# Adding the two halves of a norm's sum: small copies and an add on VectorE or GpSimd instead of a TensorE product

## The chip, the cores and the metric

The kernel runs on one core of a Trainium2 chip. The metric is device time in microseconds (us) for one execution. Before the change the median of three runs is 1548.53 us (1548.2 to 1552.75). The profile comes from one further execution of 1549.24 us, of which 1547.5 us lie between its first and its last instruction (the span).

## What is computed

A linear attention over 8 batches, 8 heads, 576 positions and a head size of 64, with a norm over the head size, and behind it two feed-forward layers over 4608 tokens (width 512, hidden width 2048). All is float32.

```
kv  = einsum('bhsd,bhse->bhde', k, v)
out = einsum('bhsd,bhde->bhse', q, kv)
rms = sqrt(mean(out * out, axis=-1, keepdims=True) + 1e-06)
x   = out / rms * g_norm          # as [4608, 512]
h = x @ moe_w_in;   r = maximum(h, 0);   x = (s * (r * r) + b) @ moe_w_out
h = x @ moe2_w_in;  x = (h / (1 + exp(-h))) @ moe2_w_out
```

## The kernel before

The tokens are cut into nine blocks of 512 columns: block t holds the first 512 positions of batch t, and the ninth block (t = 8) the remaining 64 positions of all eight batches. Products that need float32 are made of three passes with each operand split into a rounded half and a rest (mm3, lines 207 to 210).

Attention goes by pairs of heads: four pairs for each batch (attention_pair). For each pair TensorE makes kv (L532), the output o (L208 to L210 into o_ps) and the output of the last 64 positions (L566 into r_ps, copied out to orem by ScalarE or VectorE, L231 or L233). Then normalize follows, with two heads of 64 on the 128 partitions:

- sq (L628, ScalarE) squares o;
- part (L633, VectorE) adds the squares over groups of 32 partitions. It leaves 128 x 16 numbers, in which a head's sum is spread over two groups of 32 partitions;
- ms (L640, TensorE) adds the two groups of each head: a product with the constant matrix pairs_of, 128 x 128 by 128 x 16, into PSUM;
- rms (L644, ScalarE) takes the root, inv (L647, VectorE) the reciprocal, spread (L652, VectorE) turns it back to 128 x 512, and x (L659, VectorE) multiplies.

normalize runs 36 times: for the four pairs of batch 0 (where the flag z is true), for 28 pairs of batches 1 to 7, and four times for the ninth block (last_block). The four of batch 0 lie in the first 30 us, the other 32 between 50 us and 450 us.

In the same stretch TensorE works on blocks 0 to 4 of the first layer (unit: mm1 into h, mm2 into acc, both by L208 to L210), while ScalarE, VectorE and GpSimd turn the squares (L786, L789, L216, L222), decode weights (L309 to L332) and build sums and differences of weight quarters (L399, L413, L214, L220). From about 450 us on the other blocks go in pairs, by a scheme with seven instead of eight block products (hidden, L980; outputs, L1121 to L1123; results, L1157). The second layer's weights are decoded up to about 854 us.

The order on every engine is worked out before the launch by a planner (class Plan). Each step is added with its engines and a duration for each, a key, what it needs and makes, and the buffers it takes and gives back. The planner walks through time with these durations; a step goes to the engine on which it can start first, or, where the duration is marked Port, on which it ends first, and steps marked Port aren't planned beside one another. Each engine then runs its own list strictly in that order. So another step or another duration early in the program can change every list behind it.

PSUM tiles of the pool `at` (two buffers) are taken by a pair's kv, by the o of batches 1 to 7, by r and by ms. Before the change ms took a buffer of this pool, so it could wait until an earlier one had been copied out.

Of the kernel before, what the change touches and what calls it, by code (L numbers as in the profile page):

```python
# [8 lines left out]
F32 = mybir.dt.float32  # L9
F32R = mybir.dt.float32r  # L10
U32 = mybir.dt.uint32
AF = mybir.ActivationFunctionType
ALU = mybir.AluOpType
# [6 lines left out]
class Plan:  # L20
# [19 lines left out]
    def add(self, engines, key, fn, needs=(), makes=(), takes=(), gives=(), move=None, opens=(), until=None):  # L40
        self.ops.append((key, len(self.ops), engines, fn, needs, makes, takes, gives, move, opens, until))
        for b in gives:
            self.users[b] = self.users.get(b, 0) + 1
# [90 lines left out]
def kernel(  # L134
# [21 lines left out]
    nc = tc.nc  # L156
    B, H, S, D = q.shape
    NT, DM = out.shape
    DFF = w_in1.shape[1]
    P = 128  # L160
# [4 lines left out]
    T = NCH * P  # L165
    REM = S - T
    Q = 32
# [28 lines left out]
    ap = st_ap.enter_context(tc.tile_pool(name="ap", bufs=1))  # L196
    dr = ctx.enter_context(tc.tile_pool(name="dr", bufs=1, space=bass.MemoryType.DRAM))
    ps = ctx.enter_context(tc.tile_pool(name="ps", bufs=1, space=bass.MemoryType.PSUM))
    eng = {"PE": nc.tensor, "ACT": nc.scalar, "DVE": nc.vector, "POOL": nc.gpsimd, "SP": nc.sync}
# [24 lines left out]
    def copy(e, dst, src, factor=None):  # L224
        if factor is not None:
            if e == "ACT":
                nc.scalar.activation(dst, src, AF.Identity, scale=factor)  # L227
            else:
                eng[e].tensor_scalar(dst, src, factor, None, op0=ALU.mult)
        elif e == "ACT":  # L230
            nc.scalar.copy(dst, src)  # L231
        else:
            eng[e].tensor_copy(dst, src)  # L233

    def dma(dst, src):
        nc.sync.dma_start(out=dst, in_=src)  # L236
# [10 lines left out]
    add = plan.add  # L247
    ACT, DVE, POOL = "ACT", "DVE", "POOL"

    def psum(b, name):  # L250
        return ps.tile([P, T], F32, tag=plan.place[b], name=name)
# [10 lines left out]
    def act(n):  # L262
        return {ACT: 0.1 + n * 0.83e-3}

    def dve(n):
        return {DVE: 0.07 + n * 1.05e-3}
# [176 lines left out]
    def new_x(t):  # L443
        x_t[t] = xp.tile([P, KD, T], F32, tag="x32", name="x32")
# [3 lines left out]
    def attention_pair(bb, p, key, before=None):  # L448
# [150 lines left out]
        else:  # L599
# [14 lines left out]
        add({"SP": 0.48}, key + 2.4, lambda e: dma(orem_d[:, p, bb, :], st["orem"]), needs=[f("ro")],  # L614
            makes=[f("orem")], gives=[b["orem"]], move=0.18)
        normalize(bb, p, key + 2, [f("o")], [b["pso"]] + [b["qT"]] * z, lambda: st["pso"])

    def normalize(t, p, key, needs, gives, src):

        z = t == 0  # L620
        st = {}
        me = (t, p)
        f = lambda name: (name, t, p)
        psm = ("at", ("m", me))

        def sq(e):
            st["sq"] = lent["z", p][:, :T] if z else ap.tile([P, T], F32, tag="sq", name="sq")
            nc.scalar.activation(st["sq"], src(), AF.Square)  # L628

        def part(e):  # L630

            st["part"] = ap.tile([P, T // Q], F32, tag="part", name="part", bufs=2)
            nc.vector.tensor_reduce(  # L633
                out=st["part"], in_=st["sq"].rearrange("p (b r) -> p b r", r=Q), op=ALU.add,
                axis=mybir.AxisListType.X, apply_transpose=True,
            )

        def ms(e):
            st["ps"] = psum(psm, "m_ps")
            nc.tensor.matmul(st["ps"][:, :T // Q], pairs_of, st["part"], start=True, stop=True)  # L640

        def rms(e):
            st["rms"] = ap.tile([P, T // Q], F32, tag="rms", name="rms", bufs=2)
            nc.scalar.activation(st["rms"], st["ps"][:, :T // Q], AF.Sqrt, bias=eps, scale=1.0 / D)  # L644

        def inv(e):
            nc.vector.reciprocal(st["rms"], st["rms"])  # L647

        def spread(e):

            st["inv"] = st["sq"]
            nc.vector.transpose(  # L652
                st["inv"].rearrange("p (b d) -> p b d", d=Q), st["rms"].unsqueeze(2).to_broadcast([P, T // Q, Q])
            )

        def x(e):
            if t < TP and p == 0:
                new_x(t)
            nc.vector.scalar_tensor_tensor(  # L659
                out=x_t[t][:, p] if t < TP else st["sq"], in0=src(), scalar=gn, in1=st["inv"], op0=ALU.mult, op1=ALU.mult  # L660
            )

        add(act(T), key, sq, needs=needs, makes=[f("sq")], takes=[] if z else [("sq", me)])
        add(dve(T), key + 0.2, part, needs=[f("sq")], makes=[f("part")], takes=[("part", me)])
        add({"PE": 0.2}, key + 0.4, ms, needs=[f("part")], makes=[f("ms")], takes=[psm], gives=[("part", me)])
        add({ACT: 0.16}, key + 0.5, rms, needs=[f("ms")], makes=[f("rms")], takes=[("rms", me)], gives=[psm])
        add({DVE: 0.17}, key + 0.6, inv, needs=[f("rms")], makes=[f("inv")])
        add(dve(T), key + 0.7, spread, needs=[f("inv")], makes=[f("spread")], gives=[("rms", me)])
        add(dve(T), key + 0.8, x, needs=[f("spread"), ("gn",)] + ([("x32", t, p - 1)] if p else []), makes=[("x32", t, p)],
            takes=[("x32", t)] if t < TP and p == 0 else [], gives=[("sq", me)] * (0 < t < TP) + gives)  # L670
        if t >= TP:
            add({"SP": 0.48}, key + 0.9, lambda e: dma(x1_d[t - TP, :, p], st["sq"]), needs=[("x32", t, p)], makes=[("x1", t, p)],
                gives=[("sq", me)], move=0.73)

    def last_block(key):
        t = NB - 1
        for p in range(NP):
            st = {}
            qb = ("qT", (t, p))

            def load(e, p=p, st=st):
                st["x"] = ap.tile([P, S], F32, tag="qT", name="qT")
                dma(st["x"][:, :T], orem_d[:, p].rearrange("p b s -> p (b s)"))

            add({"SP": 0.48}, key - 1 + p * 0.1, load, needs=[("orem", bb, p) for bb in range(B)] + [("xl", t, p - 1)] * (p > 0),
                makes=[("xl", t, p)], takes=[qb], move=0.73)
            normalize(t, p, key + 0.5 + 0.7 * p, [("xl", t, p)], [qb], lambda st=st: st["x"][:, :T])
# [502 lines left out]
    with tc.manual_schedule():  # L1190
# [5 lines left out]
        eps, gn, s_t, b_t, sgn, mag_s, root, guess, b1, b_neg, g0 = (vecs[:, i:i + 1] for i in range(11))  # L1196
# [19 lines left out]
        for i in range(2):  # L1216
            nc.vector.tensor_tensor(
                pairs_of.rearrange("p (h i d) -> p h i d", h=2, d=Q)[:, :, i], quarters[:, :, 0], quarters[:, :, 1],
                op=ALU.add,
# [40 lines left out]
        for m in range(KF):  # L1260
            for kind in "io":
                to, tag = wanted[2 * m + (kind == "o")], f"w{kind}{m}"
# [19 lines left out]
        def turn2(e):  # L1282
# [4 lines left out]
            needs=[("x1", t, p) for p in range(NP) for t in range(TP, NB)] + [("x32", NB - 1, p) for p in range(NP)], makes=[("l2p",)],  # L1287
            gives=[("xr", x) for x in P_RING])
# [6 lines left out]
        for b_, x in new + [(("xr", x), x) for x in P_RING]:  # L1295
            plan.settle(b_, x)
        add({POOL: 0.0}, KF * (TP - 2) + 12, turn3,
            needs=[("wd", n, l, kind, j) for n in range(8) for l in range(2) for kind in "io" for j in range(NS) if (n, l) != (A21, 0)],
            makes=[("l2q",)], gives=[b_ for b_, _ in new])
# [23 lines left out]
        for i in range(350):  # L1323
            add({"PE": 0.11 * (2 if i < 17 else 1)}, 1e6 + i,
                warm_up,
                takes=[("acc", "warm")] * (i == 0), gives=[("acc", "warm")], until=40)
# [51 lines left out]
```

## Time and profile before

| | |
|---|---|
| median of three runs | 1548.53 us |
| the profiled execution, and its span | 1549.24 us, 1547.5 us |
| TensorE busy | 1536.7 us (99%) |
| VectorE, ScalarE, GpSimd busy | 70%, 55%, 41% |
| DMA engines, mean | 233 GB/s |
| TensorE's share of the chain that ended last | 88% |

An engine's busy time is the union of its instructions' records. A matmul's end is modelled: one of 512 columns is drawn 0.39 us long while the next starts 0.23 us later, so the distance of two starts is what a matmul costs. PEld is the loading of weights into TensorE; it runs beside the matmul in front. A float32 product that isn't split by the program stands as two loads and two matmuls, so the 32 products of the change are 64 records.

### The profile page before, as it was taken

What the parts mean: (1) busy time and instruction counts of PE and PEld (TensorE: products, weight loads), DVE (VectorE), ACT (ScalarE), POOL (GpSimd) and SP (SyncE); (2) the same over time, 40 slices, a digit from 0 to 9 for tenths busy, and PEclk for the clock granted to TensorE, in tenths of its full rate; (3) what the DMA queues carried; (4) which work ended last, traced back from release to release, by engine and by line L of the source; (5) the groups of instructions that cost most, each with busy time, mean ns of one, the idle gap of its engine ahead of it and who ended that gap; (6) DMA issues with size and microseconds to landing.
All of it is one profiled execution on the core that took longest, in us unless ns stands there. A gap on an engine that the chain in (4) does not pass through costs nothing.

```text
span 1547.5 us, 23039 instructions
## 1 busy us (share of the span) xinstructions
PE 1536.7 (99%) x7402; PEld 1255.4 (81%) x7402; DVE 1084.1 (70%) x1908; ACT 855.9 (55%) x1683; POOL 634.4 (41%) x584
## 2 busy tenths in 40 slices
PE   9999999999999999999999999999999999999999
PEld 6778888887888888888888788888888888888887
DVE  6887787877677587888888766765676666666521
ACT  6886566566576586667665444544444344544222
POOL 2331122111125144578457823762376246622410
PEclk9999999999999999999999999999999999999999
DMA  8866789988466788897988876877677766876684
GB/s 220 214 188 197 218 253 285 280 233 243 164 217 231 254 254 261 281 310 249 333 277 289 259 239 192 264 189 252 190 258 189 250 196 218 189 254 200 198 197 150
DMA packets 343496, 361.22 MB, mean 233 GB/s; under 512 B 166480, under 2 KB 228944, under 8 KB 343376
## 3 DMA queue, kind: packets, MB, share of 16 engines
q1 hardware_dynamic: 343248, 359.76, 76.4%
q8 instruction: 59, 0.97, 0.3%
q14 instruction: 61, 0.50, 0.1%
q0 software_dynamic: 128, 0.00, 0.0%
HBM read 272.63 MB, written 87.03 MB: 232 GB/s over the span
## 4 chain that ended last, share of the span: by engine, by line
PE 88%; DMA 4%; DVE 3%; ACT 2%; SPq 1%; issue 1%; POOL 1%; POOLq 0%; ACTq 0%; DVEq 0%
PE hp L980 28%; PE acc L1121 10%; PE acc L1123 10%; PE acc L1122 10%; PE h L208 5%; PE h L210 4%; PE h L209 4%; PE acc L208 4%; PE acc L209 4%; PE acc L210 4%; DMA raw<-in_moe_w_out_dram 1%; PE kv_ps L532 1%; PE acc L820 1%; PE acc L819 1%; PE acc L821 1%; SPq L236 1%
## 5 line engine op out<-in xcount | busy, mean ns | idle before, releaser
L980 PE MATMUL hp<-xo,win 128*128 128x512 f32 x2016 | 510.6, 390 | 1.8 <-DVE tmp L1005 1.8
L980 PEld LDWEIGHTS hp<-xo,win 128*128 128x128 f32 x2016 | 378.0, 188 | 84.1 <-DVE tmp L1005 5.9
L220 POOL TENSOR_TENSOR g<-tmp,g 128x512 fp32r<-128x512 f32 x192 | 249.7, 1308 | 309.4 <-ACT g L214 277.7
L1121 PE MATMUL acc<-g,wout 128*128 128x512 f32 x672 | 262.0, 390 | 0.8 <-DVE ya L1132 0.5
L1123 PE MATMUL acc<-g,wout 128*128 128x512 f32 x672 | 261.8, 390 | 0.0
L1122 PE MATMUL acc<-g,wout 128*128 128x512 f32 x672 | 261.7, 389 | 0.0
L1130 DVE TENSOR_TENSOR ya<-acc,ya 128x512 f32<-128x512 f32 x168 | 115.6, 688 | 126.9 <-PE acc L1123 117.8
L1121 PEld LDWEIGHTS acc<-g,wout 128*128 128x128 f32 x672 | 126.1, 188 | 27.9 <-DVE ya L1132 0.9
L1123 PEld LDWEIGHTS acc<-g,wout 128*128 128x128 f32 x672 | 126.3, 188 | 26.4
L1122 PEld LDWEIGHTS acc<-g,wout 128*128 128x128 f32 x672 | 126.3, 188 | 26.2
L214 ACT ACTIVATE g<-tmp 128x512 fp32r<-128x512 f32 x192 | 119.4, 629 | 26.3 <-PE acc L1123 11.7
L208 PE MATMUL acc<-gh,wo 128*128 128x512 f32 x320 | 132.2, 413 | 0.4 <-ACT y L227 0.4
L786 ACT ACTIVATE h<-h 128x512 f32<-128x512 f32 x96 | 56.0, 583 | 131.9 <-PE h L210 131.3
L208 PE MATMUL h<-xh,wi 128*128 128x512 f32 x320 | 126.7, 396 | 0.1
L1157 POOL TENSOR_TENSOR ya<-ya 128x512 f32<-128x512 f32 x84 | 108.2, 1318 | 45.1 <-DVE ya L1130 35.6
L210 PE MATMUL h<-xh,wi 128*128 128x512 f32 x320 | 125.2, 391 | 0.0
L210 PE MATMUL acc<-gh,wo 128*128 128x512 f32 x320 | 125.2, 391 | 0.0
L209 PE MATMUL acc<-gh,wo 128*128 128x512 f32 x320 | 125.1, 391 | 0.0
L209 PE MATMUL h<-xl,wi 128*128 128x512 f32 x320 | 124.9, 390 | 0.0
L332 POOL TENSOR_TENSOR rq<-raw 128x256 uint32<-128x256 uint32 x68 | 43.5, 640 | 189.5 <-DVE raw L318 101.1
L1005 DVE TENSOR_TENSOR tmp<-hp,tmp 128x512 f32<-128x512 f32 x144 | 98.8, 686 | 24.5 <-PE hp L980 23.1
L214 ACT ACTIVATE rq<-rq 128x256 fp32r<-128x256 f32 x192 | 77.5, 413 | 63.4 <-POOL rq L332 28.9
(170 smaller groups left out, 2649.4 us busy)
## 6 DMA issues: line engine op xcount, KB each, us to landing
wout<-wo SPq DMA_DIRECT2D x368, 256.0 KB, 4.2
win<-wi SPq DMA_DIRECT2D x144, 512.0 KB, 5.1
wi<-rq SPq DMA_DIRECT2D x96, 256.0 KB, 3.7
wo<-rq SPq DMA_DIRECT2D x96, 256.0 KB, 3.4
win<-wi SPq DMA_DIRECT2D x80, 256.0 KB, 4.2
raw<-in_moe_w_out_dram SPq DMA_DIRECT2D x36, 256.0 KB, 4.2
raw<-in_moe_w_in_dram SPq DMA_DIRECT2D x16, 512.0 KB, 4.8
raw<-in_moe_w_in_dram SPq DMA_DIRECT2D x32, 256.0 KB, 4.8
```

The costliest lines, as they stand in the source:

```text
L208: nc.tensor.matmul(ps, wh, xh, start=first, stop=False)
L209: nc.tensor.matmul(ps, wh, xl, start=False, stop=False)
L210: nc.tensor.matmul(ps, wl, xh, start=False, stop=last)
L214: nc.scalar.activation(hi, src, AF.Copy)
L220: eng[e].tensor_tensor(lo, src, f32(hi), op=ALU.subtract)
L980: nc.tensor.matmul(to, w[:, wn, f_], x_[:, xn], start=first and n == 0, stop=kk == KH - 1 and n == 2, skip_group_check=True)
L1005: nc.vector.tensor_tensor(t, bank[me, a], tmp[b_, me], op=ALU.add)
L1121: nc.tensor.matmul(to, w[:, 0, dd], gh, start=a == 0, stop=False)
L1122: nc.tensor.matmul(to, w[:, 0, dd], gl, start=False, stop=False)
L1123: nc.tensor.matmul(to, w[:, 1, dd], gh, start=False, stop=a == 1)
L1130: nc.vector.tensor_tensor(y2[tp, i, d], st["ps"], y2[tp, i, d], op=ALU.add)
L1157: eng[e].tensor_tensor(y2[tp, i, d], y2[tp, i, d], y2[tp, j, d], op=ALU.add)
```

## The change

For z (batch 0) nothing changes. For the other 32 norms the product ms is replaced by both_halves. It takes a tile rms, copies each group of 32 partitions of part to the neighbour's place in it (four copies of 32 x 16), and adds part (128 x 16). All five instructions go to VectorE or all to GpSimd, as the planner decides with 0.5 us or 0.8 us, both marked Port. The root then reads rms in SBUF and writes it in place; its planned duration goes from 0.16 to 0.2 us. No buffer of `at` is taken.

```diff
+        def both_halves(e):
+            st["rms"] = ap.tile([P, T // Q], F32, tag="rms", name="rms", bufs=2)
+            for i in range(P // Q):
+                j = i ^ 1
+                copy(e, st["rms"][i * Q:(i + 1) * Q], st["part"][j * Q:(j + 1) * Q])
+            eng[e].tensor_tensor(st["rms"], st["rms"], st["part"], op=ALU.add)
...
-            nc.scalar.activation(st["rms"], st["ps"][:, :T // Q], AF.Sqrt, bias=eps, scale=1.0 / D)
+            nc.scalar.activation(st["rms"], st["ps"][:, :T // Q] if z else st["rms"], AF.Sqrt, bias=eps, scale=1.0 / D)
...
-        add({"PE": 0.2}, key + 0.4, ms, needs=[f("part")], makes=[f("ms")], takes=[psm], gives=[("part", me)])
-        add({ACT: 0.16}, key + 0.5, rms, needs=[f("ms")], makes=[f("rms")], takes=[("rms", me)], gives=[psm])
+        if z:
+            add({"PE": 0.2}, key + 0.4, ms, needs=[f("part")], makes=[f("ms")], takes=[psm], gives=[("part", me)])
+        else:
+            add({DVE: Port(0.5), POOL: Port(0.8)}, key + 0.4, both_halves, needs=[f("part")], makes=[f("ms")], takes=[("rms", me)], gives=[("part", me)])
+        add({ACT: 0.2}, key + 0.5, rms, needs=[f("ms")], makes=[f("rms")], takes=[("rms", me)] * z, gives=[psm] * z)
```

The planner gives 27 of the 32 sets to VectorE and 5, all early ones, to GpSimd, and it works out all lists anew: the first row that differs is row 103 on TensorE, 62 on VectorE, 16 on GpSimd and 11 on ScalarE.

TensorE's list at the second pair of batch 1, behind the product of the last positions (r_ps); acc and h are the first layer's products. Before:

```order
L566 MATMUL r_ps<-qT,kvf_130 128x64
L208 MATMUL acc<-gh,wo_936 128x512
L209 MATMUL acc<-gh,wo_936 128x512
L210 MATMUL acc<-gh,wo_936 128x512
L640 MATMUL m_ps<-part,pairs_of 128x16
L208 MATMUL acc<-gh,wo_936 128x512
```

and after:

```order
L566 MATMUL r_ps<-qT,kvf_130 128x64
L208 MATMUL acc<-gh,wo_874 128x512
L209 MATMUL acc<-gh,wo_874 128x512
L210 MATMUL acc<-gh,wo_874 128x512
L208 MATMUL h<-xh,wi_910 128x512
L209 MATMUL h<-xl,wi_910 128x512
```

The product is gone from the stream of three-pass products, and the pair comes one unit earlier among them (its neighbours use an earlier weight tile).

VectorE's list at the first pair of batch 1, from its sum over partitions (L633) to the reciprocal (L647 before, L655 after); gh is the rest of the first layer's hidden values, wi and wo are weights. Before:

```order
L633 TENSOR_REDUCE part<-sq 128x16
L222 SCALAR_TENSOR_TENSOR gh<-h,vecs,gh 128x512
L313 TENSOR_SCALAR raw<-raw 128x512
L220 TENSOR_TENSOR qTl<-qT,qTh 128x512
L647 RECIPROCAL rms<-rms 128x16
```

and after:

```order
L633 TENSOR_REDUCE part<-sq 128x16
L222 SCALAR_TENSOR_TENSOR gh<-h,vecs,gh 128x512
L233 COPY rms<-part 32x16 x4
L647 TENSOR_TENSOR rms<-rms,part 128x16
L313 TENSOR_SCALAR raw<-raw 128x512
```

Four copies and an add stand in front of the weights' decoding now.

GpSimd's list from its last memset on; L332 are the sums of the weights' decoding. Before:

```order
L1212 MEMSET kvf_130 128x128
L332 TENSOR_TENSOR dw<-raw 128x512 x30
L332 TENSOR_TENSOR rq<-raw 128x256 x4
L413 TENSOR_TENSOR rq<-rq 128x256 x2
L399 TENSOR_TENSOR rq<-wo_542 128x256
```

and after:

```order
L1223 MEMSET kvf_130 128x128
L332 TENSOR_TENSOR dw<-raw 128x512 x13
L233 COPY rms<-part 32x16 x4
L647 TENSOR_TENSOR rms<-rms,part 128x16
L332 TENSOR_TENSOR dw<-raw 128x512 x14
L233 COPY rms<-part 32x16 x4
L647 TENSOR_TENSOR rms<-rms,part 128x16
```

Two of GpSimd's five sets stand among the thirty sums of the first decoding.

## Rows read from the trace of the kernel before

**Rows 1.** The page, part 1: busy us, share of the span, instructions.

```profile
PE 1536.7 (99%) x7402; PEld 1255.4 (81%) x7402; DVE 1084.1 (70%) x1908; ACT 855.9 (55%) x1683; POOL 634.4 (41%) x584
```

**Rows 2.** Stretches: their us, then busy us of PE, PEld, DVE, ACT, POOL; PEclk, DMA.

```profile
30.00:100.00 70.00, 69.38 (x391) 54.61 (x390) 61.43 (x109) 59.51 (x117) 22.85 (x21) 1.00 0.79 207
...
30.00:460.00 430.00, 428.14 (x2387) 344.12 (x2386) 336.06 (x696) 290.55 (x640) 97.44 (x118) 1.00 0.77 226
...
830.00:880.00 50.00, 47.58 (x201) 38.24 (x200) 37.71 (x59) 22.96 (x45) 42.12 (x39) 0.97 0.84 270
...
880.00:1548.00 668.00, 663.65 (x2921) 546.92 (x2920) 398.59 (x610) 277.37 (x476) 285.52 (x224) 1.00 0.72 215
```

**Rows 3.** TensorE's timeline at an undelayed product: start us, us drawn, line, tiles, count.

```profile
90.22 0.39 PE L210 MATMUL acc<-gh,wo 128*128 128x512 f32 x1
90.44 0.29 PE L640 MATMUL m_ps<-part,pairs_of 128*128 128x16 f32 x2
90.58 0.48 PE L208 MATMUL acc<-gh,wo 128*128 128x512 f32 x1
90.90 0.40 PE L209 MATMUL acc<-gh,wo 128*128 128x512 f32 x1
```

**Rows 4.** The product's tile, 30 to 460 us: PE with idle time before, then PEld.

```profile
L640 PE MATMUL m_ps<-part,pairs_of x64: 177/262/283, 55.2 to 446.4; 128*128 128x16 f32 x64
...
  DVE orem L233: 0.8, 2
  ACT kvf L231: 0.3, 1
...
  DVE orem L233: 1.7, 2
  DVE part L633: 1.0, 2
  ACT kvf L231: 0.9, 2
  ACT orem L231: 0.6, 1
```

**Rows 5.** Timeline of one delayed product, with the copy that it waited for.

```profile
70.66 0.40 PE L210 MATMUL acc<-gh,wo 128*128 128x512 f32 x1
...
71.41 0.22 DVE L233 COPY orem<-r_ps 128x64 f32<-128x64 f32 x1
...
71.68 0.40 PE L640 MATMUL m_ps<-part,pairs_of 128*128 128x16 f32 x2 [0.62 <-DVE orem L233]
```

**Rows 6.** VectorE's small instructions: four of the timeline, one group (busy, mean ns).

```profile
4.69 0.15 DVE L1222 TENSOR_SCALAR vecs<-vecs 128x1 f32<-128x1 f32 x1 [0.18 <-DMA vecs<-in_moe_s_dram]
4.88 0.15 DVE L1223 TENSOR_SCALAR vecs<-vecs 128x1 f32<-128x1 f32 x1
...
21.42 0.09 DVE L1233 TENSOR_TENSOR vecs<-vecs 128x1 f32<-128x1 f32 x1
21.56 0.15 DVE L1234 TENSOR_SCALAR vecs<-vecs 128x1 f32<-128x1 f32 x1
...
L647 DVE RECIPROCAL rms<-rms 128x16 f32<-128x16 f32 x36 | 8.8, 244 | 8.8 <-ACT rms L644 8.7
```

**Rows 7.** GpSimd's groups: its smallest instruction, and its smallest sum (busy, mean ns).

```profile
L1362 POOL MEMSET const-float32-0.0<- 128x1 f32 x1 | 0.1, 99 | 0.2 <-issue 0.2
...
L332 POOL TENSOR_TENSOR rq<-raw 128x256 uint32<-128x256 uint32 x68 | 43.5, 640 | 189.5 <-DVE raw L318 101.1 <-DMA wo<-rq 15.9 <-DVE raw L328 14.0
```

**Rows 8.** VectorE beside GpSimd: min/median/max ns of one line; timeline around 870 us.

```profile
L413 DVE TENSOR_TENSOR rq<-rq x88: 357/419/1511, 144.3 to 868.5; 128x256 f32<-128x256 f32 x88
...
869.36 6.97 POOL L1157 TENSOR_TENSOR ya<-ya 128x512 f32<-128x512 f32 x5
870.22 3.75 DVE L220 TENSOR_TENSOR rq<-rq 128x256 fp32r<-128x256 f32 x3
...
874.63 0.97 PE L980 MATMUL hp<-xo,win 128*128 128x512 f32 x3 [1.60 <-DVE tmp L1005]
```

More of the change, by code (lines that the diff above doesn't have):

```diff
@@ L640, in ms @@
             nc.tensor.matmul(st["ps"][:, :T // Q], pairs_of, st["part"], start=True, stop=True)
+        def both_halves(e):
[4 more added lines that the diff above has]
+            eng[e].tensor_tensor(st["rms"], st["rms"], st["part"], op=ALU.add)
         def rms(e):
-            st["rms"] = ap.tile([P, T // Q], F32, tag="rms", name="rms", bufs=2)
-            nc.scalar.activation(st["rms"], st["ps"][:, :T // Q], AF.Sqrt, bias=eps, scale=1.0 / D)
+            if z:
+                st["rms"] = ap.tile([P, T // Q], F32, tag="rms", name="rms", bufs=2)
+            nc.scalar.activation(st["rms"], st["ps"][:, :T // Q] if z else st["rms"], AF.Sqrt, bias=eps, scale=1.0 / D)
         def inv(e):
@@ L664, in normalize @@
         add(dve(T), key + 0.2, part, needs=[f("sq")], makes=[f("part")], takes=[("part", me)])
-        add({"PE": 0.2}, key + 0.4, ms, needs=[f("part")], makes=[f("ms")], takes=[psm], gives=[("part", me)])
-        add({ACT: 0.16}, key + 0.5, rms, needs=[f("ms")], makes=[f("rms")], takes=[("rms", me)], gives=[psm])
+        if z:
+            add({"PE": 0.2}, key + 0.4, ms, needs=[f("part")], makes=[f("ms")], takes=[psm], gives=[("part", me)])
+        else:
+            add({DVE: Port(0.5), POOL: Port(0.8)}, key + 0.4, both_halves, needs=[f("part")], makes=[f("ms")], takes=[("rms", me)], gives=[("part", me)])
+        add({ACT: 0.2}, key + 0.5, rms, needs=[f("ms")], makes=[f("rms")], takes=[("rms", me)] * z, gives=[psm] * z)
         add({DVE: 0.17}, key + 0.6, inv, needs=[f("rms")], makes=[f("inv")])
```

## The prediction

> **What bounds the kernel now.** I read the page first: TensorE is busy 99% of the span and no other engine more than 70% [rows 1]. A busy TensorE may still hide idle time, so I went on to the stretches. From 30 to 460 us, where all 32 norms of the change lie, TensorE is busy for 428.14 of 430 us at the full granted clock, VectorE for 336.06 (78%), GpSimd for 97.44 (23%) [rows 2]. So TensorE sets the time there, and whatever leaves its list shortens the run, as long as nothing else becomes late. The one later place where it visibly loses time is 830 to 880 us: 2.42 us idle and a granted clock of 0.97 on average [rows 2]. I come back to it, since the change works out all lists anew.
>
> **What a product costs on TensorE.** The drawn 0.29 us is no price; the starts are [rows 3]. With no product in between, two starts lie 0.22 to 0.23 us apart (I use 0.227 for a matmul of 512 columns). From the matmul at 90.22 to the second one behind the product, at 90.90, is 0.68 us, and the two matmuls of 512 columns in it take 0.454. The product thus takes 0.226 us: 0.14 between its first start and the next matmul's, and some 0.09 by which the following matmul's slot is longer (0.32 instead of 0.23). The price is nearly that of a full matmul, though only 16 columns go through. There are 64 records, so 32 products [rows 4]: 32 x 0.226 = **7.2 us removed**.
>
> The Trainium skill speaks against this price: "TensorE: Matmul & The Clock Gate", section "Back-to-back issue gap", gives a matmul of 1 to 64 columns about 60 cycles, an issue floor of some 25 ns. By that page two matmuls are 50 ns and 32 products 1.6 us. The trace disagrees, with 0.226 us for one product, and I go by the trace; the page's result stands below as a rival.
>
> **What the products made TensorE wait for.** The product takes a buffer of the PSUM pool that the copy of the last positions (orem) or of kv has to empty first. One case is plain: the matmul before starts at 70.66, the copy at 71.41, the product at 71.68, a distance of 1.02 us instead of 0.23 [rows 5]. Over all 32 products TensorE idles 1.1 us in front of the matmuls (three times) and 4.2 us in front of their loads (seven times) [rows 4]. The second sum holds time in which the matmul before still ran, so the true loss lies between the two, 1.1 to 4.2 us. Without the product nothing asks for that buffer until the next pair, so I expect the waits to go: **2.5 us removed**, with 0 (another instruction waits in the product's place) and 4.2 as ends.
>
> **What is added.** 27 sets of four copies and an add go on VectorE, 5 on GpSimd. No row has a copy of 32 x 16 in SBUF. From below: two neighbours of 128 x 1 start 0.14 us apart, five of them 0.7 us. From above: the reciprocal of 128 x 16 is drawn 0.244 us long, five of them 1.2 us. I take the 0.19 us between the starts at 4.69 and 4.88, where the second needs the first, as the add needs the copies [rows 6]: 0.95 us for a set, 26 us in all. VectorE goes from 336 to 362 us of 430, or 84%. On GpSimd an instruction lies between 0.099 us (memset of 128 x 1) and 0.640 (sum of 128 x 256) [rows 7], nearer to the first with its 16 columns. I take 0.2, so 1 us for a set; the ends are 0.5 and 3.2. GpSimd is idle for 77% of the stretch, which covers it.
>
> Behind a set on VectorE wait the decoding of weights and the rests of the hidden values (L222), for which TensorE's second product waits. This is where the added time could reach the path. It costs nothing if the remaining 68 us of idle VectorE take it up. At worst the sets count in full where VectorE has the least room: 30 to 100 us, 61.43 of 70 us busy [rows 2]. The products run from 55.2 to 446.4 us [rows 4], one in 12.6 us on average, so about four fall there, 3.8 us. TensorE idles only 1.86 us of 430 in the trace of before, so VectorE's present lateness hardly reaches it, and I stay near the lower end: **1.5 us added**, between 0 and 3.8. The norm's own chain gets no price: x is wanted by the next pair's o and by the next block, and the product itself often stood in TensorE's list behind other work.
>
> ScalarE's root reads SBUF instead of PSUM and keeps its place behind a wait: nothing.
>
> **The lists behind.** All engines' lists change, into the second layer's decoding too. The lost time at 830 to 880 us shows what such a list can cost. GpSimd runs L1157 without a break from 869.36, and three sums of VectorE with both inputs in SBUF take 3.75 us together [rows 8]. One sum of that size takes 0.42 us in the median and up to 1.51 [rows 8]. VectorE's next copies come late, TensorE idles 1.60 us [rows 8], and its granted clock falls after the idle time. The stretch costs 2.42 us idle and 0.03 x 50 = 1.5 us of clock, 3.9 us in all [rows 2]. The Trainium skill has the rule ("GPSIMD Engine Reference", section "Key points"): GpSimd shares its SBUF interfaces with VectorE instructions that have two SBUF inputs or run in a two-port mode. By that rule the trace agrees, with 3.75 us for three sums. In the new lists such a meeting may vanish, stay or come twice; I take 0, with -3.9 and +3.9 as ends.
>
> **Sum.** The profiled execution took 1549.24 us: 1549.24 - 7.2 - 2.5 + 1.5 = 1541.0. It lies 0.7 us above the median of the runs, which gives **1540.3 us**. A difference under about 0.3% (4.6 us) can't be told from none here; the bounds are 1543.9 and 1553.2.
>
> **Rivals.**
> 1. VectorE takes the gain back. The copies queue in front of L222, and each may also be held by GpSimd by up to 1.1 us (1.51 - 0.42, rows 8). If nine of the 27 sets delay TensorE by their 0.95 us, 8.6 us are paid instead of 1.5, and the time is 1547.4. For it: 88% busy from 30 to 100 us. Against it: 78% over the stretch and 1.86 us of idle TensorE.
> 2. A product is cheap, and the next matmul's longer slot stays because something else causes it. With 25 ns a matmul, 1.6 us go instead of 7.2, and the time is 1545.9. Rows 3 speak against it: the longer slot stands right behind the product.
> 3. The meeting at 870 us vanishes as well: 1540.3 - 3.9 = 1536.4. For it: the lists there change. Against it: the work there is the same, with VectorE busy 37.71 and GpSimd 42.12 of 50 us [rows 2], so a meeting is easily replaced by another.
> 4. Slower: the new lists put VectorE's sums beside GpSimd's long runs at several places of the second layer's decoding, each for 3.9 us. The bound of 1553.2 lies 12.9 us above the forecast, so it decides from the fourth extra stretch on; four give 1540.3 + 15.6 = 1555.9. Against it: the trace of before has one such stretch, and from 880 us on TensorE idles only 4.35 us of 668 [rows 2].
>
> That the products don't leave the list is excluded by the lists themselves.
>
> **How the numbers follow.** Forecast 0.57, rival 1 0.17, rival 2 0.05, rival 3 0.13, rival 4 0.08. The forecast's own range is 1537.1 (waits 4.2, added cost 0) to 1545.1 (waits 0, added cost 3.8); about nine tenths of it lie under 1543.9, so 0.51 of its chance is faster. With rival 3 and a little of rival 1 that makes 0.66 faster. Within 0.3% are the forecast's rest, most of rival 1 and rival 2: 0.25. Slower are rival 4 and a worse rival 1: 0.09. The range reaches from 1534.0 (rival 3 with the better waits) to 1549.0 (the forecast's upper end and one more stretch of 3.9 us); rival 4 lies outside.
>
> **What would show it.** In the profile of the changed kernel, 64 records of L640's kind less on TensorE, a stretch from batch 1 to the last norm that is some 8 to 9 us shorter, and starts 0.23 us apart where the products stood, confirm the first two terms. A set of about 0.95 us on VectorE and VectorE's share near 84% there confirm the third; TensorE idle with L222 as releaser means rival 1. Idle TensorE and a fallen clock behind long sums of VectorE, at 860 us or elsewhere, mean that the lists decided. The prediction is wrong if that stretch gets shorter as expected and the time is given back behind it, or if small copies cost VectorE over 2 us a set.

## The result: slower by 0.59%

The changed kernel takes 1559.2 us (median of seven runs, 1555.2 to 1563.5), beside 1548.5 us for the kernel before. The ratio is 1.0059, with a 95% interval from 1.0044 to 1.0074, or about +9.1 us. The forecast was 1540.3 us, and the range ended at 1549.0.

The profiled execution is the fastest of the seven (1555.2 us), so its trace shows 6 of the 9 us. Some 1.4 of these 6 stand in its first 28 us, where the granted clock fell once (0.94 on average, 1.00 in the profile of before). Two runs with the old lists have the same fall there, so the fall isn't the change's. This is the page's first part of the changed kernel:

```profile
PE 1532.5 (99%) x7338; PEld 1250.1 (80%) x7338; DVE 1102.7 (71%) x2034; ACT 855.4 (55%) x1690; POOL 641.9 (41%) x611
```

The 64 records of the products are gone (7402 to 7338), as in [rows 1] without them. TensorE is busy 4.2 us less and the span is 5.9 us longer (1553.4), so TensorE idles some 10 us more. The stretches tell where; their us stand first, then busy us of PE, PEld, DVE, ACT and POOL, the granted clock and the DMA's share:

```profile
30.00:100.00 70.00, 69.05 (x406) 53.58 (x405) 60.23 (x111) 60.20 (x122) 22.97 (x26) 1.00 0.79 214
30.00:460.00 430.00, 420.00 (x2314) 335.89 (x2313) 354.62 (x821) 289.28 (x642) 102.90 (x141) 1.00 0.76 224
460.00:830.00 370.00, 367.16 (x1609) 302.57 (x1608) 287.56 (x497) 245.05 (x484) 196.82 (x189) 1.00 0.82 267
830.00:900.00 70.00, 68.94 (x302) 56.16 (x301) 55.87 (x86) 35.58 (x68) 57.47 (x51) 1.00 0.87 283
```

From 30 to 460 us TensorE idles 10.00 us, where it idled 1.86 [rows 2]. VectorE is busy 354.62 us instead of 336.06. Behind 460 us little changes on balance: one wait of 2.35 us at 561 us is new, with a granted clock of 0.50 behind it, and the lost time at 870 us [rows 8] has become less (1.06 us idle from 830 to 900 us, where it was 2.42 from 830 to 880 [rows 2]):

```profile
561.20 5.07 PE L991 MATMUL hp<-xo,win 128*128 128x512 f32 x14 [2.35 <-DVE tmp L1016]
...
561.50:564.50 3.00, 3.00 (x8) 2.33 (x8) 1.27 (x3) 3.00 (x7) 1.28 (x1) 0.50 0.03 8
```

The new idle time of TensorE from 30 to 460 us, by what ended it (us in total, times, longest):

```profile
PE r_ps L566 <- DVE qT L546: 2.1, 2, 1.8
PE o_ps L208 <- DVE x L667: 1.5, 2, 1.2
PE o_ps L209 <- DVE qTl L220: 1.1, 1, 1.1
PE kv_ps L532 <- DVE orem L233: 1.1, 1, 1.1
PE acc L208 <- ACT gh L216: 1.1, 1, 1.1
PE h L210 <- DVE wi L220: 0.9, 2, 0.6
```

Five of these six end with VectorE. A set itself takes what was forecast (min/median/max ns of the changed kernel's tile rms):

```profile
L233 DVE COPY rms<-part x108: 161/167/921, 56.6 to 435.2; 32x16 f32<-32x16 f32 x108
...
L647 DVE TENSOR_TENSOR rms<-rms,part x27: 174/175/178, 57.3 to 435.4; 128x16 f32<-128x16 f32 x27
L233 POOL COPY rms<-part x20: 186/191/463, 69.3 to 352.3; 32x16 f32<-32x16 f32 x20
```

Most sets on VectorE last 0.915 us from the first copy to the end of the add; three are longer (1.3 to 1.8 us), and beside each of these runs a sum of GpSimd. GpSimd's five sets lie between 69 and 353 us, so they are not all early.

### The profile page after: what moved, and what is told of

Same layout as the page of the kernel before. It is cut to its first block, busy times and chain, and to the rows that moved or that the text cites. A ratio compares the mean times of both kernels' runs of the same rounds, so it can differ in the third digit from the quotient of the medians.

```text
span 1553.4 us, 23076 instructions
## 1 busy us (share of the span) xinstructions
PE 1532.5 (99%) x7338; PEld 1250.1 (80%) x7338; DVE 1102.7 (71%) x2034; ACT 855.4 (55%) x1690; POOL 641.9 (41%) x611
## 4 chain that ended last, share of the span: by engine, by line
PE 65%; DVE 1%; POOL 1%; DMA 1%; ACT 0%; issue 0%; DVEq 0%; POOLq 0%; ACTq 0%
PE hp L991 28%; PE acc L1132 9%; PE acc L1134 9%; PE acc L1133 9%; PE h L210 1%; PE h L209 1%; PE h L208 1%; PE acc L832 1%; PE acc L831 1%; PE acc L830 1%; PE acc L209 1%; PE acc L210 1%; PE acc L208 1%; POOL g L220 0%; POOL xo L220 0%; DVE rq L220 0%
## 5 line engine op out<-in xcount | busy, mean ns | idle before, releaser
L220 POOL TENSOR_TENSOR g<-tmp,g 128x512 fp32r<-128x512 f32 x192 | 249.2, 1305 | 304.6 <-ACT g L214 271.3
L332 POOL TENSOR_TENSOR rq<-raw 128x256 uint32<-128x256 uint32 x68 | 44.0, 648 | 181.8 <-DVE raw L318 109.7
```

Source lines behind the costliest of these rows:

```text
L220: eng[e].tensor_tensor(lo, src, f32(hi), op=ALU.subtract)
```

## The experiments

Two theories stood against each other at first. V: VectorE's time for the sets reaches TensorE. L: the planner's new lists are worse, whatever the sets cost. The change does three things at once (a product less, a set more, new lists), so the first runs take them apart. Ratios are to the kernel before, run beside each, with a 95% interval; a gain or loss in us is the ratio less 1, times 1549. A price that is taken from two of these ratios has a wider interval, which stands behind it; where it reaches zero, the price isn't shown. A draw means one set of lists that the planner happens to make.

### The sets in the old lists

The step keeps its duration, buffer and place in the plan, so every list is that of before, except for the instructions themselves.

```diff
         def ms(e):
-            st["ps"] = psum(psm, "m_ps")
-            nc.tensor.matmul(st["ps"][:, :T // Q], pairs_of, st["part"], start=True, stop=True)
+            if z:
+                st["ps"] = psum(psm, "m_ps")
+                nc.tensor.matmul(st["ps"][:, :T // Q], pairs_of, st["part"], start=True, stop=True)
+            else:
+                both_halves(DVE)
...
         add({"PE": 0.2}, key + 0.4, ms, needs=[f("part")], makes=[f("ms")], takes=[psm], gives=[("part", me)])
```

> Planned as before (the step keeps TensorE's 0.2 us, its buffer and its place), but in the product's place the four copies and the add are issued on VectorE; every list is that of before except for these. Theory V (VectorE's time: a set takes 0.83 to 0.92 us on VectorE, which makes what TensorE waits for late): as slow as the changed kernel, 1555 to 1562 us. Theory L (the new lists: without the product the planner orders everything anew, and TensorE waits at other places): 1539 to 1544 us, the forecast's gain.

Measured: 1551.6 us, ratio 1.0015 (1.0004 to 1.0027), +2.3 us. It lies between the theories. Without new lists the change is slower too, but by a quarter of the loss. The stretch of this kernel:

```profile
30.00:460.00 430.00, 423.44 (x2332) 337.26 (x2331) 363.65 (x859) 292.14 (x642) 96.62 (x119) 1.00 0.77 225
```

### The old lists with nothing in the product's place

```diff
         def ms(e):
-            st["ps"] = psum(psm, "m_ps")
-            nc.tensor.matmul(st["ps"][:, :T // Q], pairs_of, st["part"], start=True, stop=True)
+            if z:
+                st["ps"] = psum(psm, "m_ps")
+                nc.tensor.matmul(st["ps"][:, :T // Q], pairs_of, st["part"], start=True, stop=True)
...
-            nc.scalar.activation(st["rms"], st["ps"][:, :T // Q], AF.Sqrt, bias=eps, scale=1.0 / D)
+            nc.scalar.activation(st["rms"], st["ps"][:, :T // Q] if z else st["part"], AF.Sqrt, bias=eps, scale=1.0 / D)
```

> Planned as before, but the 32 products are left out and nothing takes their place; the root reads the unadded sums, so the norm lacks the other half. It prices the product with its waits. V and L: 1537 to 1542 us (7.2 us of products and up to 4 us of waits less). If a product costs next to nothing: 1545 to 1548 us.

Measured: 1545.0 us, ratio 0.9970 (0.9959 to 0.9981), -4.6 us. The products with their waits are worth 4.6 us (2.9 to 6.4), not 9.7. By the time alone a product could cost next to nothing, as the last expectation has it. The trace of before says otherwise: read from the starts as in [rows 3], 25 of the 32 products take 0.225 to 0.252 us each, and all 32 with their waits 10.4 us. TensorE's stretch and its waits from 30 to 460 us in this kernel:

```profile
30.00:460.00 430.00, 424.71 (x2343) 340.59 (x2342) 338.14 (x703) 291.14 (x645) 98.32 (x119) 1.00 0.78 227
...
PE acc L208 <- ACT y L227: 1.7, 1, 1.7
PE o_ps L209 <- DVE qTl L220: 0.9, 1, 0.9
PE kv_ps L532 <- DMA rem_t<-in_v_dram: 0.7, 1, 0.7
PE h L208 <- ACT wi L214: 0.7, 1, 0.7
```

TensorE idles 5.29 us instead of 1.86, though the 1.1 us in front of the products [rows 4] are gone. The wait for a copy of y behind a DMA was 0.4 us before; those for a rest of q, for a load and for a weight are new. Freed of the products TensorE comes earlier to steps whose other engines don't come earlier. With the sets added (the run before this one) the price of 32 sets on VectorE follows: 0.0045, or 7.0 us (4.5 to 9.5).

### The new lists without the sets

```diff
         def both_halves(e):
             st["rms"] = ap.tile([P, T // Q], F32, tag="rms", name="rms", bufs=2)
-            for i in range(P // Q):
...
-            eng[e].tensor_tensor(st["rms"], st["rms"], st["part"], op=ALU.add)
...
-            nc.scalar.activation(st["rms"], st["ps"][:, :T // Q] if z else st["rms"], AF.Sqrt, bias=eps, scale=1.0 / D)
+            nc.scalar.activation(st["rms"], st["ps"][:, :T // Q] if z else st["part"], AF.Sqrt, bias=eps, scale=1.0 / D)
```

> Planned as the changed kernel, but the copies and the add are left out; the root reads the unadded sums, so the norm lacks the other half. It prices the sets in the new lists. Theory V: most of the loss goes, 1540 to 1549 us. Theory L: the loss stays, 1553 to 1559 us.

Measured: 1548.7 us, ratio 0.9994 (0.9984 to 1.0004), -0.9 us. Most of the loss goes with the sets, as V has it: they cost 0.0065, or 10 us (7 to 13), in these lists. But L has a share: the same work takes 0.0024, or 3.7 us (1.4 to 6.0), longer in the new lists than in the old. In the profiled executions this difference lies for the most part behind the norms. These are the stretches of this kernel, then one of the run before without sets:

```profile
30.00:460.00 430.00, 423.67 (x2336) 339.13 (x2334) 335.99 (x689) 292.67 (x655) 102.31 (x120) 1.00 0.76 226
460.00:830.00 370.00, 367.16 (x1608) 302.19 (x1607) 290.20 (x501) 243.47 (x478) 197.59 (x188) 1.00 0.82 269
557.00:560.00 3.00, 3.00 (x9) 2.32 (x8) 1.49 (x4) 3.00 (x6) 0.83 (x2) 0.50 0.54 150
PE hp L987 <- DVE tmp L1012: 2.3, 1, 2.3
...
460.00:830.00 370.00, 369.70 (x1627) 304.84 (x1627) 294.24 (x503) 248.81 (x485) 203.60 (x190) 1.00 0.82 270
```

Up to 460 us TensorE idles 6.33 us in the new lists and 5.29 in the old, from there to 830 us 2.84 and 0.30. The greater part is the one wait for a sum of VectorE (L1012) near 555 us, with the fall of the clock behind it, which the changed kernel has at 561 us.

### The sets' real duration told to the planner

```diff
-            add({DVE: Port(0.5), POOL: Port(0.8)}, key + 0.4, both_halves, ...
+            add({DVE: Port(0.85), POOL: Port(1.2)}, key + 0.4, both_halves, ...
```

> The changed kernel with the durations that the trace shows: the planner is told 0.85 us (VectorE) and 1.2 us (GpSimd) for a set instead of 0.5 and 0.8. Theory V in its mild form (not the set's time but its being planned too short makes the lists run late): 1540 to 1548 us. Theory L: another draw of lists, anywhere from 1541 to 1560 us, with no reason to be better.

Measured: 1554.1 us, ratio 1.0031 (1.0021 to 1.0042), +4.8 us. It is better than the change, but the mild form of V wanted 1548 at most. That a set is planned too short is not the main cause; and as these are other lists again, what is gained can't be put down to the duration.

### The product and, besides, the sets

The old lists with the products; the sets are issued on VectorE at the same place into a tile that nothing reads.

```diff
             nc.tensor.matmul(st["ps"][:, :T // Q], pairs_of, st["part"], start=True, stop=True)
+            if not z:
+                extra = ap.tile([P, T // Q], F32, tag="extra", name="extra", bufs=2)
+                for i in range(P // Q):
+                    j = i ^ 1
+                    copy("DVE", extra[i * Q:(i + 1) * Q], st["part"][j * Q:(j + 1) * Q])
+                nc.vector.tensor_tensor(extra, extra, st["part"], op=ALU.add)
```

> The kernel before with its product and all its lists, and besides the four copies and the add on VectorE at the product's place, into a tile that nothing reads. It prices 32 sets of 0.83 to 0.92 us on VectorE alone. Theory V (VectorE is near its limit in this stretch, so its time reaches TensorE): 1554 to 1558 us. Rival S (the sets cost only because TensorE, freed of the products, runs ahead into VectorE; with the products there is room): 1549 to 1552 us.

Measured: 1553.6 us, ratio 1.0026 (1.0013 to 1.0038), +4.0 us: just under V's interval and over S's. The sets cost 4 us (2.0 to 5.9) even where no result waits for them and the products keep TensorE back; that is V's part. The 7 us without the products lie 2.9 us higher (-0.2 to 6.1), so that TensorE's running ahead adds to the price isn't shown.

### The sets on GpSimd, in the old lists

```diff
-                both_halves(DVE)
+                both_halves(POOL)
```

> Planned as before, with the copies and the add in the product's place on GpSimd instead of VectorE. Theory V: GpSimd is idle for three quarters of the stretch, so most of the sets' 7 us goes: 1545 to 1548 us. Rival C (a set costs because it lengthens the norm's own chain, on whichever engine): 1551 to 1555 us, since a set takes 1.0 to 1.9 us on GpSimd.

Measured: 1546.4 us, ratio 0.9980 (0.9971 to 0.9989), -3.1 us. It beats both kernels, by little. The sets cost 0.0010, or 1.5 us (-0.7 to 3.7), on GpSimd and 7.0 on VectorE, though they are longer there: 1.4 us in the median from the first copy to the end of the add. The norm's chain isn't longer: from the end of part to the start of the root go 2.4 us in the median, as before the change, and 3.1 with the sets on VectorE, where they queue. So this run alone doesn't part VectorE's time from the chain. Two others do: the run before cost 4.0 us though no result waited for the sets, and in the changed kernel this way is shorter than before, 1.4 us, and the time longer. What costs is mainly VectorE's time.

### Other lists with the product

The kernel before, with nothing changed but the duration that the planner assumes for the product: 0.3, 0.1 and, in a later run, 0.22 us.

```diff
-        add({"PE": 0.2}, key + 0.4, ms, ...
+        add({"PE": 0.3}, key + 0.4, ms, ...
```

> The kernel before with nothing changed but the planner's duration of the product, 0.3 instead of 0.2 us, which gives other lists. Theory L in its general form (another draw of the lists moves the time by several us, without any work changed): outside 1546 to 1552 us. Theory V: lists alone matter little, 1547 to 1551 us.

> As the run before, with 0.1 us as the product's duration: a second draw of lists. Theory L: outside 1546 to 1552 us, and elsewhere than the run with 0.3. Theory V: 1547 to 1551 us.

> The kernel before with the product's planned duration at 0.22 instead of 0.2 us: a third draw of the lists, nearer to those of before (TensorE's list is the same for its first 199 rows). If the lists of before are an unusually good draw, as the draws with 0.3 and 0.1 suggest: 1552 to 1559 us. If those two were unlucky and draws lie on both sides: 1545 to 1552 us.

Measured: 1558.4 us with 0.3 (1.0058, 1.0039 to 1.0077), 1557.2 us with 0.1 (1.0049, 1.0034 to 1.0064), 1551.5 us with 0.22 (1.0014, 1.0003 to 1.0025). The same instructions in another order cost 9.0, 7.6 and 2.2 us. All three draws are slower than the lists of before. The draw with 0.22, which resembles the old lists most, loses least.

### All sets on GpSimd, with new lists

```diff
-            add({DVE: Port(0.5), POOL: Port(0.8)}, key + 0.4, both_halves, ...
+            add({POOL: Port(1.2)}, key + 0.4, both_halves, ...
```

> The change with all 32 sets on GpSimd, planned there with 1.2 us, so that the planner draws new lists without the product. If the parts add up (product -4.6 us, sets on GpSimd +1.5, a draw of lists +4 to +9): 1550 to 1556 us. If the changed kernel is slow mainly because of VectorE's sets, and its lists are no worse than others: 1545 to 1549 us.

Measured: 1551.6 us, ratio 1.0008 (0.9997 to 1.0019), +1.2 us. It is slower than the same sets in the old lists by 0.0028, or 4.3 us (2.1 to 6.5), as the sum of the parts has it.

### Product and sets in a second set of lists

The lists of the run with 0.3 us, once with nothing in the product's place and once with the sets on VectorE there (the edits of the first two runs).

> The lists of the run with the product planned at 0.3 us, with the 32 products left out and nothing in their place; the root reads the unadded sums, so the norm lacks the other half. It prices the product in a second set of lists. If a product taken from TensorE is worth about half its 10 us wherever it stands (the rest comes back as other waits): 4 to 6 us below that run's 1558.4, so 1552 to 1555 us. If the old lists alone hid its worth: 8 to 11 us below, 1547 to 1550 us.

> The same lists with the copies and the add on VectorE in the product's place: the change without new lists, in the second set of lists. If the parts add up as in the old lists (sets +7, product -4.6): 1559 to 1563 us, 0 to 4 above the run with the product. If VectorE has more room in these lists, where TensorE waits more: 1553 to 1558 us.

Measured: 1554.0 us without the product (1.0022, 1.0009 to 1.0034), 1567.0 us with the sets (1.0108, 1.0089 to 1.0128). Taken from the run with the product, 1.0058, the product is worth 5.6 us (2.1 to 9.1), about as in the old lists. The sets cost 0.0086, or 13.3 us (9.7 to 16.9), more than either expectation. Here 11 of the 32 sets stand beside a sum of GpSimd and last 1.3 to 2.7 us; in the old lists it was six, up to 2.0 us. Together the sets last 38 us here and 33.5 there. VectorE's idle share doesn't tell the two lists apart: without the sets it is busy 334 us of 430 here and 338 in the old lists.

This pair shows the way from VectorE to TensorE best. TensorE's idle time by releaser up to 130 us, first without the sets:

```profile
PE h L210 <- DVE wi L220: 1.2, 2, 0.8
PE h L208 <- ACT wi L214: 0.8, 1, 0.8
PE r_ps L566 <- ACT lent_wi L231: 0.5, 1, 0.5
```

and with them:

```profile
PE h L210 <- DVE wi L220: 4.6, 3, 2.5
PE r_ps L566 <- ACT lent_wi L231: 0.8, 1, 0.8
PE h L208 <- ACT wi L214: 0.2, 1, 0.2
```

One of the three waits, on the timeline with the sets (start us, us, engine, line, tiles):

```profile
75.64 0.99 DVE L318 SCALAR_TENSOR_TENSOR raw<-dw,raw 128x512 uint32<-128x512 uint32 x1
76.66 1.45 DVE L233 COPY rms<-part 32x16 f32<-32x16 f32 x4
76.86 1.04 POOL L332 TENSOR_TENSOR dw<-raw 128x512 uint32<-128x512 uint32 x1 [0.78 <-ACT wi L214]
78.14 0.17 DVE L650 TENSOR_TENSOR rms<-rms,part 128x16 f32<-128x16 f32 x1
78.24 0.42 DVE L313 TENSOR_SCALAR raw<-raw 128x512 uint32<-128x512 uint32 x1
78.57 0.68 DVE L220 TENSOR_TENSOR wi<-dw,wi 128x512 fp32r<-128x512 f32 x1
...
79.31 0.50 PE L210 MATMUL h<-xh,wi 128*128 128x512 f32 x1 [1.25 <-DVE wi L220]
```

The four copies last 1.45 us instead of 0.7, since GpSimd's sum of 1.04 us runs beside them. Behind the set stands the rest of a weight (wi, L220), and TensorE has idled 1.25 us when it gets it. The longest of the three waits goes the same way, with two sums of GpSimd beside the set:

```profile
97.78 2.49 DVE L233 COPY rms<-part 32x16 f32<-32x16 f32 x4
...
100.40 0.68 DVE L220 TENSOR_TENSOR wi<-dw,wi 128x512 fp32r<-128x512 f32 x1
...
101.14 0.50 PE L210 MATMUL h<-xh,wi 128*128 128x512 f32 x1 [2.55 <-DVE wi L220]
```

The third, of 0.8 us at 123.5 us, comes in another way: VectorE itself waits 2.30 us for a norm's root before it makes the rest of the weight. VectorE runs its list in order, so a set that nobody needs at once delays a result that TensorE needs now. The stretches from 30 to 460 us, first without and then with the sets:

```profile
30.00:460.00 430.00, 420.58 (x2317) 336.04 (x2316) 334.11 (x696) 288.84 (x642) 103.86 (x121) 1.00 0.77 225
...
30.00:460.00 430.00, 413.51 (x2289) 328.73 (x2287) 355.74 (x828) 279.66 (x621) 100.06 (x118) 1.00 0.75 218
```

TensorE's idle time goes from 9.42 to 16.49 us, with VectorE at 83%.

## Why the prediction was wrong

The loss goes from the kernel before to the changed one in three measured steps: product out, old lists, -4.6 us; sets on VectorE, old lists, +7.0 us; the planner's own lists (five of the sets on GpSimd there), +6.8 us. They add up to the measured +9.1 (9.2 by rounding) by their making, since each is taken from the same ratios; each is uncertain by 2 to 3 us. The forecast had -9.7, +1.5 and 0 in their places, so it missed by 5.1, 5.5 and 6.8 us.

1. **"TensorE sets the time there, and whatever leaves its list shortens the run."** This step failed first. The spacing was read rightly (10.4 us with the waits, over all 32), but the 9.7 us taken from TensorE were worth 4.6 in the old lists, and the products 5.6 in another set. Being busy for 428.14 of 430 us [rows 2] says that TensorE rarely waits, not that the others have time to spare: the lists keep them only just ahead of it. A TensorE that is faster by 0.3 us in each of 32 norms meets the next wait (1.86 to 5.29 us of idle time).
2. **"1.5 us added, between 0 and 3.8."** The duration was right where no sum of GpSimd runs beside the set (0.95 forecast, 0.915 measured; up to 2.7 us beside one), and so was VectorE's load (84% forecast, 82.5% measured). The cover was not: 18% of idle time on average hid little of a set, since VectorE's list is in order and what TensorE needs next stands behind the set. The sets cost 7.0 us in the old lists, 13.3 in the second ones, and 4.0 beside the products. The upper end came from the 70 us in which VectorE is fullest; the waits of the changed kernel lie all along the stretch.
3. **"The lists behind: I take 0, with -3.9 and +3.9 as ends."** The new lists cost 3.7 us without the sets, at the edge of this, and 6.8 with them. Behind 460 us zero came out, but by luck: the time lost at 870 us shrank, and a new wait at 561 us, with a fall of the clock, lost about as much. That wait is for a sum of VectorE which lasts its usual 0.68 us, so it isn't GpSimd that holds it up. What is lost on top with the sets lies mostly in the attention's own stretch, where I looked for no price of the lists: TensorE idles 6.56 us there with the sets in the old lists and 10.00 in the new. Three other draws with all the old work cost 2.2 to 9.0 us. The old lists are better than each of the draws that were tried, and zero was the wrong middle for a change that draws anew.
4. **Rival 1** had the mechanism of the second step, the sets that GpSimd holds up included, and nearly its size (8.6 us). TensorE waited less for L222 than for other results of VectorE, though (0.3 us of the 10.00). It ended at 1547.4 because it kept the first step. **Rival 2** named nearly the worth that was measured for the products, 1.6 us and the waits, but for a reason that didn't hold: the products did take their 0.226 us. **Rival 4** had the sign and not the mechanism: no long run of GpSimd behind 460 us was needed.

Of what was to show the steps, the 64 records less and the set of 0.95 us on VectorE came true. The stretch that was to be 8 to 9 us shorter is so by its ends, and misleads: the norms' additions run from 55.2 to 446.4 us before [rows 4] and from 56.6 to 435.4 us after, some 12 us less, only because the new lists place the last norm earlier among the rest. Up to 460 us TensorE idles 8 us more. The lower end of the range, 1534.0, comes out as 1534.7 from its own terms (1536.4 less 1.7 us of waits); nothing rests on it.

What makes the old lists good is open. The draws differ from them in hundreds of places, and no run here changed one place alone. The new lists also place the attention otherwise (the last pair's o ends near 424 instead of 398 us); the price of that wasn't tried. Nor did a run part what a set costs by its bare 0.9 us from what it costs while GpSimd holds it up.

## What to carry to other kernels

An engine that is busy 99% of a stretch isn't the only limit when a planner has fitted the others closely to it: don't price an instruction taken from it at its full spacing (here about half came back as other waits), but make a run with the instruction simply left out. Small work moved to an engine that runs in order is priced by what stands behind it in the list, not by that engine's idle share; try the engine with the most room first, here GpSimd. Where an edit makes a planner order everything anew, measure the edit in the old order as well, and two or three draws of the order without the edit.

## What the runs showed of the hardware

A wait of TensorE can cost more than its length. In the changed kernel a wait for VectorE's turn of q ends at 420.63 us; soon after, the granted clock is 0.50 (1.2 instead of 2.4 GHz) from 421.5 to 424.5 us:

```profile
418.44 0.39 PE L210 MATMUL acc<-gh,wo 128*128 128x512 f32 x1
420.63 0.43 PE L566 MATMUL r_ps<-qT,kvf 128*128 128x64 f32 x2 [1.80 <-DVE qT L546]
...
421.87 0.63 PE L208 MATMUL h<-xh,wi 128*128 128x512 f32 x1
422.30 0.63 PE L209 MATMUL h<-xl,wi 128*128 128x512 f32 x1
...
421.50:424.50 3.00, 3.00 (x9) 2.32 (x8) 1.14 (x3) 0.00 (x0) 0.73 (x1) 0.50 0.87 300
```

The starts lie 0.43 us apart instead of 0.23, for seven matmuls, so some 1.4 us come on top of the two that were waited. Before the change this happened once within the layers, at 877 us. Not every wait of this length does it: behind the wait of 2.55 us at 101.14 us, in the second set of lists with the sets, the clock stays at its upper level:

```profile
101.50:104.50 3.00, 3.00 (x15) 2.47 (x14) 2.97 (x5) 2.65 (x5) 0.00 (x0) 1.00 0.37 150
```

Copies of 32 x 16 on VectorE, one after the other, start 0.18 us apart, and one of them took up to 0.92 us while GpSimd added beside it; in the second set of lists up to 1.2 us, and an add of 128 x 16 up to 0.70:

```profile
L233 DVE COPY rms<-part x128: 161/168/1203, 58.7 to 463.8; 32x16 f32<-32x16 f32 x128
...
L650 DVE TENSOR_TENSOR rms<-rms,part x32: 174/175/704, 60.2 to 464.0; 128x16 f32<-128x16 f32 x32
```

In both traces every set over 1 us has a sum of GpSimd beside it, and no shorter set meets one for more than 0.16 us. The Trainium skill states that GpSimd shares its SBUF interfaces with VectorE instructions in a two-port mode or with two SBUF inputs ("GPSIMD Engine Reference", section "Key points"); by that rule the trace agrees for the add, which has two inputs in SBUF, with 0.70 us beside a sum of GpSimd and 0.175 without. A copy has one input, and no row shows whether it runs in a two-port mode; it is held up all the same, 0.92 us beside a sum and 0.17 without. A product of 16 columns in float32 had cost TensorE nearly as much as one of 512 columns in one pass [rows 3].
